# Cluster attention and two mixers on one core: grouping the v products, packing U's products, dividing the copies of turned exponentials two to one

## The chip, the cores and the metric

The kernel runs as one program on one core of a Trainium2 chip. The metric is the device time of one execution in microseconds; smaller is better. A time given below is a median over the runs shown, unless the text says that it is that of the profiled execution.

## What is computed

Inputs are q, k, v (2 batches, 8 heads, 768 positions, 64 channels), cluster centroids, and the weights of two mixer blocks. The first part is attention in which a query sees only the keys of its own cluster; its output, 2 x 768 x 512, goes through a low-rank token mixer and a wide channel mixer, and then through a second mixer pair.

```python
q_assign = argmax(q_n . c_n)                 # nearest centroid of each query, k_assign the same
mask   = q_assign[:, :, :, None] == k_assign[:, :, None, :]
scores = where(mask, q @ k.T / 8, -1e9)
x      = softmax(scores) @ v                 # 2 x 768 x 512
u      = x + U-V token mixer:  h = x.T @ U @ V,  u = x + h.T        (rank 32)
x2     = u + relu(u @ w_ch1) @ w_ch2         # hidden width 2048
...                                          # a second mixer: 256 over tokens, 1536 over channels
```

## The kernel before

The order of all work is written out by hand (a manual schedule): each engine runs its instructions in the order in which the program issues them, and a semaphore wait in front of one holds up everything behind it on that engine.

**Attention.** Heads are taken two at a time: G = 8 pairs (4 per batch). A pair has 12 score tiles of 128 queries by 768 keys (two halves of the queries, two heads, three tiles each), so there are 96 tiles, and `step(n)` issues tile n's share. For a tile, TensorE makes the scores (`s_mm`, four matmuls of 384 columns into two PSUM banks, issued two tiles ahead), VectorE finds the row maximum (`s_max`, L289), ScalarE exponentiates into the buffer `p32` (`s_exp`, L294), TensorE turns the six 128x128 blocks (`t_mm`, L311; "turned exponentials"), and every four turned blocks are one PSUM bank that VectorE or ScalarE copies to the buffer `pt` (`t_out`, L316 and L318). One and a half such groups come from a tile, so an even step begins a group (`i == 0`) and an odd step finishes one begun before it. Groups are numbered j; odd j went to VectorE and even j to ScalarE.

**The product with v.** Six tiles make a half k of a pair. While half k is made, the steps r = 0 to 5 of it issue `pv(k - 1, r)`: the product of key block r of the half before with v, for both heads, the two heads side by side in the array's columns (64 each) and accumulating in PSUM bank 7. After the sixth block ScalarE copies the bank to `osb` (`pv_out`, L326); two steps later TensorE turns it back (`merge`, L331) and VectorE divides by the row sums into `xn` (`merge_out`, L339).

**U's product.** When a pair is finished, `zmm(g)` computes U transposed times its part of x: six matmuls that fill 32 of the array's 128 columns. Two ScalarE casts and a VectorE subtraction (`zmm_out`, L354 to L356) store it as high part, high part, low part in `zst`. The last pair's runs after the attention loop in `rest_of_u`. `zadd` later adds V's product of it to x, six times per batch; for batch 0 in the loop, for batch 1 after it.

**What fixes the place of the rest.** The dictionaries `mid` and `late` hold work keyed by step: `mid` is TensorE work (merge, zmm, scores of clusters, zadd, turning of u), `late` what the other engines and the DMA queue do at the end of a step, among it the cluster assignment of the next pair, its loads, and from step 56 the conversion of the channel mixer's weights (`wide`, L96 to L109, L78, L85). PSUM banks 4 to 6 are handed out in turn by `ring()` to turned groups, merges, zmm and the like. The order inside a step was:

```python
if i == 0:   heads; run(mid); t_mm(0..4); pvs; maxima; t_mm(4..6); exps; t_out(j); pvo; run(late)
else:        t_mm(0..2); heads; maxima; t_mm(2..6); t_out(j); pvs; run(mid); exps; t_out(j+1); pvo; run(late)
```

Here `heads` is `s_mm(n+2)`, `maxima` is `s_max(n+2)`, `exps` is `s_exp(n+1)`.

**After the loop** come the last half's product with v (six blocks in a row), and the mixers as a stream of 512-column matmuls.

Of the kernel before, what the change touches and what calls it, by code (L numbers as in the profile page):

```python
# [9 lines left out]
F32 = mybir.dt.float32  # L10
# [8 lines left out]
P = 128  # L19
# [5 lines left out]
def tile_cluster_attention__then__two_mixers(  # L25
# [24 lines left out]
    pe, dve, act, pool, sp = nc.tensor, nc.vector, nc.scalar, nc.gpsimd, nc.sync  # L50
    NB, NPAIR, _, S = qT.shape
    HS = S // 2
    NS = S // P
    NT = HS // P
    D = 64
    CD = NPAIR * P
    NC = CD // P
    NFA, NFB = wa.shape[0], wb.shape[0]
    R = U.shape[1]
    DT = wt1.shape[1]  # L60
    NDT = DT // P
    G = NB * NPAIR
    NTT = 4 * NT
# [4 lines left out]
    const = ctx.enter_context(tc.tile_pool(name="const", bufs=1))  # L68
    psp = ctx.enter_context(tc.tile_pool(name="psp", bufs=1, space=bass.MemoryType.PSUM))
    ps = psp.tile([P, 8, 512], F32, name="ps")  # L70

    def mm(o, l, r, start, stop, **kw):
        pe.matmul(o, lhsT=l, rhs=r, start=start, stop=stop, **kw)  # L73

    def rnd(eng, o, i, scale=1.0):

        if eng is act:
            act.activation(o, i, AF.Copy, scale=scale)  # L78
        elif eng is dve and scale == 1.0:
            dve.tensor_copy(o, i)  # L80
        else:
            eng.tensor_scalar(out=o, in0=i, scalar1=scale, scalar2=1.0, op0=ALU.mult, op1=ALU.mult)

    def sub(eng, o, a, b):
        eng.tensor_tensor(out=o, in0=a, in1=b, op=ALU.subtract)  # L85

    f32 = lambda ap: ap.bitcast(F32)
# [35 lines left out]
    xn = fp.tile([P, NB, NPAIR, NS, P], F32, name="xn")  # L123
# [46 lines left out]
    u_sb = const.tile([P, NS, R], F32, name="u_sb")  # L170
    vst = const.tile([96, S], F32R, name="vst")
    zst = const.tile([96, NB * CD], F32R, name="zst")
    wcl = const.tile([P, 16], BF16, name="wcl")
    msk = const.tile([P, 2], F32, name="msk")

    def load_pair(g, eng=sp):
        b, p = divmod(g, NPAIR)
        eng.dma_start(Rq, qT[b, p])
        eng.dma_start(Rk, kT[b, p])
# [5 lines left out]
    held = {}  # L185

    def scores(g):
        p = g % NPAIR
        held["sc"] = bk = ring()
        for qd in range(4):  # L190
            src = (Rq, Rk)[qd // 2]
            mm(ps[32 * qd : 32 * qd + 32, bk, 0:HS], zc[:, ts(p, 32)], src[:, ts(qd % 2, HS)], True, True)
# [47 lines left out]
    def k_lo(eng, o):  # L240
        sub(eng, o.bitcast(F32R), Rk, Hk)
# [59 lines left out]
    def ring():  # L301

        banks.append(banks.pop(0))
        return banks[-1]

    def t_mm(n, c0, c1):
        for c in range(c0, c1):
            j, i = divmod(NS * n + c, 4)
            if i == 0:
                tb[j] = ring()  # L310
            pe.transpose(ps[:, tb[j], ts(i, P)], p32[n % NP32][:, ts(c, P)], ident)  # L311

    def t_out(j):
        o = pt[:, ts(j % NBL, 4 * P)]
        if j % 2:
            dve.tensor_copy(o, ps[:, tb[j], :])  # L316
        else:
            act.copy(o, ps[:, tb[j], :])  # L318

    def pv(q, c):  # L320
        for a in range(2):
            r = pt[:, ts((2 * q + a) % 4, NBL * P)].rearrange("p (t c k) -> p t c k", t=NT, c=NS)[:, :, c, :]
            mm(ps[D * a : D * a + D, OB, 0:HS], vr[q // 2 % 2][:, c, ts(a, D)], r, c == 0, c == NS - 1)
# [4 lines left out]
    def merge(q, bk=None):  # L328
        held["mg"] = bk = bk or ring()
        for t in range(NT):  # L330
            pe.transpose(ps[:, bk, ts(t, P)], osb[q % 2][:, ts(t, P)], ident)  # L331

    def merge_out(q):
        g, h = divmod(q, 2)
        b, p = divmod(g, NPAIR)
        r = rr[h]
        dve.tensor_scalar(out=r, in0=rs[q % 4], scalar1=EPS, scalar2=None, op0=ALU.add)
        dve.reciprocal(r, r)
        dve.tensor_tensor(  # L339
            out=xn[:, b, p, ts(h, NT), :].rearrange("p t (a d) -> p (t a) d", a=2),  # L340
            in0=ps[:, held["mg"], 0:HS].rearrange("p (x d) -> p x d", d=D),
            in1=r.unsqueeze(2).to_broadcast([P, 2 * NT, D]), op=ALU.mult)

    def zmm(g, bk):
        b, p = divmod(g, NPAIR)
        held["z"] = bk
        z = ps[0:R, bk, 0:P]
        for c in range(NS):
            mm(z, u_sb[:, c, :], xn[:, b, p, c, :], c == 0, c == NS - 1)

    def zmm_out(g):
        z = ps[0:R, held["z"], 0:P]
        o = zst[:, ts(g, P)]
        act.copy(o[0:32], z)  # L354
        act.copy(o[32:64], z)
        sub(dve, o[64:96], z, f32(o[0:32]))  # L356


    def zadd(b, t, bk):
        mm(ps[:, bk, :], vst[:, ts(t, P)], zst[:, ts(b, CD)], True, True)  # L360
# [211 lines left out]


    NTILE = G * NTT
    mid, late = {}, {}

    def at(d, s, f):
        d.setdefault(max(s, 0), []).append(f)

    for g in range(G):  # L580
        s0 = NTT * g
        for h in range(2):
            s = s0 + 2 * NT * h + 4 * NT + 1
            at(mid, s, lambda q=2 * g + h: merge(q))
            at(late, s, lambda q=2 * g + h: merge_out(q))
        if g + 1 < G:
            at(mid, s0 + NTT + 8, lambda g=g: zmm(g, ring()))
            at(late, s0 + NTT + 8, lambda g=g: zmm_out(g))
        n, s1 = g + 1, s0
        if 2 <= n < G:  # L590
            at(late, s1 - 8, lambda g=n: load_pair(g))
            at(mid, s1 - 5, lambda g=n: scores(g))
            at(late, s1 - 5, scores_out)
            at(late, s1 - 4, q_hi)
            at(late, s1 - 4, arg0)
            at(late, s1 - 3, lambda: arg1(pool))
            at(late, s1 - 2, k_hi)
            at(late, s1 - 2, arg2)
            at(late, s1 - 1, lambda: arg3(pool))
            at(late, s1 - 1, lambda: k_lo(pool, Rk))  # L600
            at(late, s1, arg4)
            at(late, s1, lambda: q_lo(dve, Rq))
            at(late, s1 + 1, lambda: mask_rows(pool))
            for what, s in (("hi", -2), ("lo", 1), ("mask", 2)):
                for a in range(2):
                    at(late, s1 + s, lambda g=n, a=a, w=what: stack(g, a, w, sp))
        if n < G:
            at(late, s1 + 6 if n > 1 else 1, lambda g=n: load_v(g))

    for t in range(NS):  # L610
        s = (59, 63, 69, 75, 81, 87)[t]

        def za(t=t):
            held["za"] = ring()
            zadd(0, t, held["za"])

        at(mid, s, za)
        at(late, s, lambda t=t: zadd_out(0, t, held["za"]))
# [24 lines left out]
    def step(n):  # L643
        k, r = divmod(n, 2 * NT)
        j, i = divmod(NS * n, 4)

        def run(d):
            for f in d.get(n, ()):
                f()

        def heads():
            if n + 2 < NTILE:
                s_mm(n + 2)

        def maxima():
            if n + 2 < NTILE:
                s_max(n + 2)

        def exps():
            if n + 1 < NTILE:  # L660
                s_exp(n + 1)

        def pvs():
            if k:
                pv(k - 1, r)

        def pvo():
            if k and r == 2 * NT - 1:
                pv_out(k - 1)

        if i == 0:
            heads()
            run(mid)
            t_mm(n, 0, 4)
            pvs()
            maxima()
            t_mm(n, 4, NS)
            exps()
            t_out(j)
            pvo()  # L680
            run(late)
        else:
            t_mm(n, 0, 2)
            heads()
            maxima()
            t_mm(n, 2, NS)
            t_out(j)
            pvs()
            run(mid)
            exps()  # L690
            t_out(j + 1)
            pvo()
            run(late)
# [178 lines left out]
    def rest_of_u():  # L872


        ops = [(lambda bk: zmm(G - 1, bk), lambda bk: zmm_out(G - 1))]
        u_, z_ = ([(f, o, b, t) for b in range(NB) for t in range(NS)] for f, o in ((umm, umm_out), (zadd, zadd_out)))
        order = u_[4:6] + z_[6:8] + u_[6:8]
        for i in range(8, 12):
            order += z_[i : i + 1] + u_[i - 1 : i] * (i > 8)
        order.append(u_[11])  # L880
        for f, o, b, t in order:
            ops.append((lambda bk, f=f, b=b, t=t: f(b, t, bk), lambda bk, o=o, b=b, t=t: o(b, t, bk)))
        for i in range(len(ops) + 1):
            if i:
                ops[i - 1][1](6 + (i - 1) % 2)
            if i < len(ops):
                ops[i][0](6 + i % 2)
            for _ in range((2, 1, 1, 2, 1, 1, 1)[i] if i < 7 else 4 if i > 7 else 12):
                yield
# [61 lines left out]
```

## Time and profile before

| | |
|---|---|
| median of 3 runs | 796.47 us (795.81 to 799.31) |
| the profiled execution | 796.2 us |
| its span in the profile | 794.1 us |
| busy, TensorE / VectorE / ScalarE / GpSimd | 760.7 / 488.4 / 305.6 / 156.5 us |
| attention loop, from the first product with v to the last merge | about 36 to 274 us of the span |

The profile is a page of one execution and a trace that can be asked for stretches, lines and waits. "PE" is TensorE's matmuls, "PEld" its weight loads, DVE VectorE, ACT ScalarE. fp32 matmuls appear as two records each, so a block of the product with v (two heads) is four records. The granted clock is TensorE's clock as a share of full speed. A row of a timeline that ends with a bracket tells how long the engine was idle before it and which instruction ended that.

### The profile page before, as it was taken

To read this page: it belongs to the slowest core of one execution; us is meant where nothing else is said; L and a number is where in the kernel's file an instruction comes from. 1 tells how busy PE (TensorE), PEld (TensorE's weight loads), DVE (VectorE), ACT (ScalarE), POOL (GpSimd) and SP (SyncE) were. 2 spreads that over 40 slices of the span, in tenths; PEclk is the share of its full clock that TensorE was granted. 3 is DMA by queue.
4 is the path that set the end of the run, shared out by engine and by line. 5 is a ranking of instruction groups with operands and counts; after the bars stand their busy time and mean duration, and the time that the engine had idled before them with its cause. 6 is when DMAs were issued, how large, how long until landed. Compare 5 with 4: busy or idle time off the path is not lost.

```text
span 794.1 us, 10612 instructions
## 1 busy us (share of the span) xinstructions
PE 760.7 (96%) x3845; PEld 584.4 (74%) x3845; DVE 488.4 (62%) x719; ACT 305.6 (38%) x563; POOL 156.5 (20%) x135
## 2 busy tenths in 40 slices
PE   1989999999999999899999999999999999999998
PEld 0655666666666677677788888888888888888886
DVE  5877767768877589695757887856682232114113
ACT  3566665666666444232323333323241210110110
POOL 3340430421400001141322222214411220000000
PEclk9999999999999999999999999999999999999999
DMA  5962644566621158999999899978775437555752
GB/s 148 214 128 81 139 113 129 126 207 152 165 92 54 54 212 292 392 368 353 391 386 326 302 392 375 377 282 277 267 282 206 134 133 246 203 187 169 273 193 80
DMA packets 59204, 176.66 MB, mean 222 GB/s; under 512 B 8625, under 2 KB 16817, under 8 KB 57105
## 3 DMA queue, kind: packets, MB, share of 16 engines
q1 hardware_dynamic: 58640, 175.27, 66.0%
q10 hardware_dynamic: 512, 0.72, 0.3%
q8 instruction: 30, 0.49, 0.2%
q14 instruction: 22, 0.17, 0.1%
HBM read 124.58 MB, written 32.51 MB: 198 GB/s over the span
## 4 chain that ended last, share of the span: by engine, by line
PE 86%; DMA 6%; DVE 3%; ACT 2%; issue 1%; ACTq 0%; SPq 0%; DVEq 0%
PE ps L73 76%; PE ps L311 8%; DMA qk<-scr_a 4%; PE ps L331 1%; DMA sk__80<-in_kT_dram 1%; DVE c__75 L106 1%; PE ps L823 1%; DVE c__75 L109 1%; DMA sq__79<-in_qT_dram 1%; ACT qk L78 1%; DMA qk<-sq__79 0%; PE ps L368 0%; ACT p L294 0%; DMA qk<-om 0%; DVE gl L729 0%
## 5 line engine op out<-in xcount | busy, mean ns | idle before, releaser
L73 PE MATMUL ps<-gh,qk 128*128 128x512 f32 x672 | 221.8, 391 | 3.3 <-DMA qk<-scr_a 3.2
L729 DVE SCALAR_TENSOR_TENSOR gl<-ps,gh 128x512 fp32r<-128x512 f32 x84 | 58.0, 690 | 190.7 <-ACT gh L728 190.7
L728 ACT ACTIVATE gh<-ps 128x512 fp32r<-128x512 f32 x84 | 50.2, 598 | 274.6 <-PE ps L73 274.1
L73 PEld LDWEIGHTS ps<-gh,qk 128*128 128x128 f32 x672 | 126.2, 188 | 30.6 <-ACT c__75 L96 2.7
L73 PE MATMUL ps<-qk 112*128 112x384 f32 (+2 forms) x492 | 119.6, 371 | 12.1 <-DMA qk<-om 9.7
L73 PE MATMUL ps<-gl,qk 128*128 128x512 f32 x336 | 130.9, 390 | 0.0
L289 DVE TENSOR_REDUCE nm<-ps 128x1 f32<-128x768 f32 x96 | 91.7, 955 | 41.0 <-PE ps L73 39.5
L73 PEld LDWEIGHTS ps<-qk 112*128 112x128 f32 (+1 forms) x492 | 84.6, 192 | 37.3 <-ACT p L294 14.3
L311 PEld LDWEIGHTS ps<-ident,p 128*128 128x128 f32 x576 | 67.0, 141 | 35.4 <-issue 19.3
L85 POOL TENSOR_TENSOR qk<-c__75,qk 128x512 fp32r<-128x512 f32 x34 | 49.1, 1449 | 222.9 <-ACT qk L78 220.3
L311 PE MATMUL ps<-ident,p 128*128 128x128 f32 x576 | 89.5, 278 | 2.4 <-ACT p L294 1.5
L294 ACT ACTIVATE p<-ps,nm 128x768 f32<-128x768 f32 x96 | 86.6, 902 | 11.2 <-DVE nm L289 10.6
L73 PE MATMUL ps<-pt,vr 128*64 128x384 f32 x384 | 82.1, 510 | 0.0
L73 PE MATMUL ps<-u1h,qk 128*128 128x512 f32 x224 | 73.9, 391 | 0.1
L73 PE MATMUL ps<-u2h,qk 128*128 128x512 f32 x224 | 73.9, 391 | 0.0
L73 PEld LDWEIGHTS ps<-gl,qk 128*128 128x128 f32 x336 | 63.1, 188 | 12.5
L318 ACT COPY pt<-ps 128x512 f32<-128x512 f32 x72 | 42.1, 585 | 70.7 <-PE ps L311 69.3
L73 PE MATMUL ps<-qk,qk 128*128 128x512 f32 x228 | 55.9, 394 | 1.0 <-DMA qk<-scr_a 1.0
L73 PEld LDWEIGHTS ps<-qk,qk 128*128 128x128 f32 x228 | 42.2, 188 | 10.0 <-DMA qk<-scr_a 1.4
L316 DVE COPY pt<-ps 128x512 f32<-128x512 f32 x72 | 49.0, 681 | 0.4 <-PE ps L311 0.4
L73 PEld LDWEIGHTS ps<-u1h,qk 128*128 128x128 f32 x224 | 42.0, 188 | 9.1 <-DMA qk<-scr_a 0.5
L73 PEld LDWEIGHTS ps<-u2h,qk 128*128 128x128 f32 x224 | 42.0, 188 | 8.6
(138 smaller groups left out, 906.9 us busy)
## 6 DMA issues: line engine op xcount, KB each, us to landing
qk<-scr_a SPq DMA_DIRECT2D x84, 512.0 KB, 7.9
qk<-scr_b SPq DMA_DIRECT2D x72, 512.0 KB, 4.2
c__74<-in_wa_dram SPq DMA_DIRECT2D x16, 1024.0 KB, 6.2
c__74<-in_wb_dram SPq DMA_DIRECT2D x24, 512.0 KB, 6.7
scr_b<-qk SPq DMA_DIRECT2D x24, 512.0 KB, 6.5
scr_a<-qk SPq DMA_DIRECT2D x22, 512.0 KB, 4.9
qk<-sq__79 SPq DMA_DIRECT2D x14, 384.0 KB, 4.0
qk<-sk__80 SPq DMA_DIRECT2D x28, 192.0 KB, 2.8
```

The source lines that it names most:

```text
L73: pe.matmul(o, lhsT=l, rhs=r, start=start, stop=stop, **kw)
L78: act.activation(o, i, AF.Copy, scale=scale)
L85: eng.tensor_tensor(out=o, in0=a, in1=b, op=ALU.subtract)
L106: dve.scalar_tensor_tensor(out=d, in0=lo, scalar=29, in1=d, op0=ALU.logical_shift_right, op1=ALU.bitwise_or)
L109: dve.scalar_tensor_tensor(out=d, in0=hi, scalar=-0x40000000, in1=d, op0=ALU.bitwise_and, op1=ALU.bitwise_or)
L289: dve.tensor_reduce(out=nm[:, n % 4 : n % 4 + 1], in_=ps[:, b0 : b0 + 2, 0:HS], axis=AX.XY, op=ALU.max, negate=True)
L294: act.activation(p32[n % NP32].rearrange("p (j k) -> p j k", j=2), ps[:, b0 : b0 + 2, 0:HS], AF.Exp, bias=nm[:, n % 4 : n % 4 + 1], accum_ ...
L311: pe.transpose(ps[:, tb[j], ts(i, P)], p32[n % NP32][:, ts(c, P)], ident)
L316: dve.tensor_copy(o, ps[:, tb[j], :])
L318: act.copy(o, ps[:, tb[j], :])
L728: act.activation(gh, o, AF.Relu)
L729: dve.scalar_tensor_tensor(out=gl, in0=o, scalar=0.0, in1=f32(gh), op0=ALU.max, op1=ALU.subtract)
```

## The change

Three edits, and a move that goes with the first. (1) `pv` is issued in odd steps alone, for two key blocks, r - 1 and r; in odd steps `mid` moves ahead of it, next to the transposes, and a new dictionary `low` (the cluster scores and `zmm`) runs right behind it. (2) `zmm` takes several pairs, each in its own 32 columns, at step 57 (pairs 0 to 3), step 93 (pairs 4 to 6) and after the loop (pair 7). Its results are first copied to `z32` (VectorE and ScalarE in turn) and then split for all pairs at once by `z_split` (two ScalarE roundings and one subtraction, in the two steps behind). The steps of `zadd` for batch 0 move from 59, 63, 69, 75, 81, 87 to 63, 65, 69, 71, 75, 77. (3) `t_out` gives every third group (j % 3 == 1) to VectorE and the others to ScalarE: 48 and 96 groups in all, where both had 72.

```diff
+    z32 = const.tile([32, CD], F32, name="z32")
...
     def t_out(j):
-        if j % 2:
+        if j % 3 == 1:
             dve.tensor_copy(o, ps[:, tb[j], :])
         else:
             act.copy(o, ps[:, tb[j], :])
...
-    def zmm(g, bk):
+    def zmm(gs, bk):
         held["z"] = bk
         for c in range(NS):
-            mm(z, u_sb[:, c, :], xn[:, b, p, c, :], c == 0, c == NS - 1)
+            for i, g in enumerate(gs):
+                b, p = divmod(g, NPAIR)
+                mm(ps[R * i : R * i + R, bk, 0:P], u_sb[:, c, :], xn[:, b, p, c, :], c == 0, c == NS - 1)
...
+    def zmm_out(gs):
+        for i, g in enumerate(gs):
+            z, o = ps[R * i : R * i + R, held["z"], 0:P], z32[:, ts(g % NPAIR, P)]
+            if i % 2:
+                act.copy(o, z)
+            else:
+                dve.tensor_copy(o, z)
+
+    def z_split(gs):
+        n, g = len(gs), gs[0]
+        z, o = z32[:, g % NPAIR * P : (g % NPAIR + n) * P], zst[:, g * P : (g + n) * P]
+        return [lambda: rnd(act, o[0:32], z), lambda: rnd(act, o[32:64], z), lambda: sub(dve, o[64:96], z, f32(o[0:32]))]
...
-            at(mid, s1 - 5, lambda g=n: scores(g))
+            at(low, s1 - 5, lambda g=n: scores(g))
...
+    for s, gs in ((57, range(NPAIR)), (93, range(NPAIR, G - 1))):
+        at(low, s, lambda gs=gs: zmm(gs, ring()))
+        at(late, s, lambda gs=gs: zmm_out(gs))
+        for i, f in enumerate(z_split(gs)):
+            at(late, s + (i + 3) // 2, f)
...
-        s = (59, 63, 69, 75, 81, 87)[t]
+        s = (63, 65, 69, 71, 75, 77)[t]
...
         def pvs():
             if k:
+                pv(k - 1, r - 1)
                 pv(k - 1, r)
...
             t_mm(n, 0, 4)
-            pvs()
             maxima()
...
             t_mm(n, 2, NS)
+            run(mid)
             t_out(j)
             pvs()
-            run(mid)
+            run(low)
             exps()
```

**Where the instructions stand.** First TensorE in the two steps of tiles 22 and 23 (qk are score matmuls, ident,p the turnings, pt,vr the product with v; here a matmul of either kind is one row entry). Before:

```order
L73 MATMUL ps<-qk_72 128x384 x4
L311 MATMUL ps<-ident,p_2_91 128x128 x4
L73 MATMUL ps<-pt,vr_88 64x384 x2
L311 MATMUL ps<-ident,p_2_91 128x128 x2
L311 MATMUL ps<-ident,p_3_92 128x128 x2
L73 MATMUL ps<-qk_72 128x384 x4
L311 MATMUL ps<-ident,p_3_92 128x128 x4
L73 MATMUL ps<-pt,vr_88 64x384 x2
```

The same two steps in the change:

```order
L73 MATMUL ps<-qk_72 128x384 x4
L312 MATMUL ps<-ident,p_2_91 128x128 x6
L312 MATMUL ps<-ident,p_3_92 128x128 x2
L73 MATMUL ps<-qk_72 128x384 x4
L312 MATMUL ps<-ident,p_3_92 128x128 x4
L73 MATMUL ps<-pt,vr_88 64x384 x4
```

The two groups of the product with v have become one, and tile 23's first two turnings follow those of tile 22 with nothing between.

Then ScalarE over three tiles (p buffers 0 to 2; L294 or L295 is the exponential, L318 or L319 the copy of a turned group). Before:

```order
L294 ACTIVATE p_0_89,rs_97<-ps,nm 128x768
L294 ACTIVATE p_1_90,rs_97<-ps,nm 128x768
L318 COPY pt<-ps 128x512
L294 ACTIVATE p_2_91,rs_98<-ps,nm 128x768
L318 COPY pt<-ps 128x512
```

In the change:

```order
L295 ACTIVATE p_0_89,rs_98<-ps,nm 128x768
L319 COPY pt<-ps 128x512
L295 ACTIVATE p_1_90,rs_98<-ps,nm 128x768
L319 COPY pt<-ps 128x512
L295 ACTIVATE p_2_91,rs_98<-ps,nm 128x768
L319 COPY pt<-ps 128x512
```

A copy now stands between any two exponentials.

Last, TensorE around U's product. Before, for one pair, in step 56:

```order
L73 MATMUL ps<-qk_72 128x384 x4
L73 MATMUL ps<-xn,u_sb 32x128 x6
L311 MATMUL ps<-ident,p_0_89 128x128 x4
L73 MATMUL ps<-pt,vr_87 64x384 x2
```

In the change, for four pairs, in step 57:

```order
L312 MATMUL ps<-ident,p_1_90 128x128 x4
L73 MATMUL ps<-pt,vr_87 64x384 x4
L73 MATMUL ps<-xn,u_sb 32x128 x24
L73 MATMUL ps<-qk_73 128x384 x4
```

It has moved from between scores and turnings to right behind the product with v.

## Rows read from the trace of the kernel before

**Rows 1.** The page, busy time of each engine.
```profile
PE 760.7 (96%) x3845; PEld 584.4 (74%) x3845; DVE 488.4 (62%) x719; ACT 305.6 (38%) x563; POOL 156.5 (20%) x135
```

**Rows 2.** Busy time by stretch: stretch, length, PE, PEld, DVE, ACT, POOL, clock, DMA.
```profile
48.00:284.00 236.00, 232.40 (x1442) 151.81 (x1441) 173.24 (x264) 147.12 (x290) 47.31 (x41) 1.00 0.46 119
```

**Rows 3.** Waits of TensorE, 20 to 284 us: total, times, longest.
```profile
PE ps L73 <- DMA sk__80<-in_kT_dram: 0.6, 1, 0.6
```

**Rows 4.** Timeline of PE, steps 16 and 17: start, length, engine, line, records.
```profile
62.24 0.98 PE L73 MATMUL ps<-qk 112*128 112x384 f32 x4
63.06 0.60 PE L311 MATMUL ps<-ident,p 128*128 128x128 f32 x4
63.59 0.87 PE L73 MATMUL ps<-pt,vr 128*64 128x384 f32 x4
64.38 0.66 PE L311 MATMUL ps<-ident,p 128*128 128x128 f32 x4
64.80 0.95 PE L73 MATMUL ps<-qk 112*128 112x384 f32 x4
...
66.12 0.87 PE L73 MATMUL ps<-pt,vr 128*64 128x384 f32 x4
66.91 0.97 PE L73 MATMUL ps<-qk 112*128 112x384 f32 x4
```

**Rows 5.** Timeline of PE behind the loop: the last half's six blocks.
```profile
276.12 4.09 PE L73 MATMUL ps<-pt,vr 128*64 128x384 f32 x24
280.14 0.98 PE L73 MATMUL ps<-qk 128*128 128x512 f32 x3
```

**Rows 6.** Timeline of PE at steps 2 and 3: eight turnings in a row.
```profile
29.09 1.03 PE L311 MATMUL ps<-ident,p 128*128 128x128 f32 x8
29.88 0.95 PE L73 MATMUL ps<-qk 128*128 128x384 f32 x4
```

**Rows 7.** Timeline of PE in a pair of steps with U's product.
```profile
74.59 0.96 PE L73 MATMUL ps<-qk 128*128 128x384 f32 x4
75.48 1.50 PE L73 MATMUL ps<-xn,u_sb 128*32 128x128 f32 x12
76.90 0.66 PE L311 MATMUL ps<-ident,p 128*128 128x128 f32 x4
...
80.81 0.98 PE L73 MATMUL ps<-qk 112*128 112x384 f32 x4
```

**Rows 8.** Timeline of PE: start of the cluster scores ahead of the row at 74.59.
```profile
73.80 0.52 PE L73 MATMUL ps<-sq__79,zc 128*32 128x384 f32 x2
```

**Rows 9.** Groups by shape, 20 to 420 us: count, busy, mean ns, idle before.
```profile
L289 DVE TENSOR_REDUCE nm<-ps 128x1 f32<-128x768 f32 x96 | 91.7, 955 | 41.0 <-PE ps L73 39.5 <-PE ps L311 0.9
L294 ACT ACTIVATE p<-ps,nm 128x768 f32<-128x768 f32 x96 | 86.6, 902 | 11.2 <-DVE nm L289 10.6
L316 DVE COPY pt<-ps 128x512 f32<-128x512 f32 x72 | 49.0, 681 | 0.4 <-PE ps L311 0.4
L318 ACT COPY pt<-ps 128x512 f32<-128x512 f32 x72 | 42.1, 585 | 70.7 <-PE ps L311 69.3 <-DVE qk L85 1.2
L78 ACT ACTIVATE qk<-c__75 128x1024 fp32r<-128x1024 f32 x6 | 6.3, 1057 | 2.6 <-DVE c__75 L109 2.6
```

**Rows 10.** Timeline of all engines at step 11: ScalarE's conversion of V's weights.
```profile
53.16 0.92 ACT L96 ACTIVATE xn<-xn 96x768 f32<-96x768 f32 x1
```

**Rows 11.** Timeline of all engines, steps 17 and 18: copy to osb, V's split, exponential, turning.
```profile
67.03 0.48 ACT L326 COPY osb<-ps 128x384 f32<-128x384 f32 x1 [0.22 <-PE ps L73]
67.41 2.54 ACT L78 ACTIVATE vst<-xn 32x768 fp32r<-32x768 f32 x3
...
69.97 0.90 ACT L294 ACTIVATE p<-ps,nm 128x768 f32<-128x768 f32 x1
...
71.02 0.44 PE L311 MATMUL ps<-ident,p 128*128 128x128 f32 x2 [1.53 <-ACT p L294]
```

**Rows 12.** Waits of TensorE, 284 to 794 us.
```profile
PE ps L73 <- DMA qk<-scr_a: 4.7, 4, 2.3
```

More of the change, by code (lines that the diff above doesn't have):

```diff
@@ L342, in merge_out @@
             in1=r.unsqueeze(2).to_broadcast([P, 2 * NT, D]), op=ALU.mult)
-    def zmm(g, bk):
-        b, p = divmod(g, NPAIR)
+    def zmm(gs, bk):
         held["z"] = bk
-        z = ps[0:R, bk, 0:P]
         for c in range(NS):
-            mm(z, u_sb[:, c, :], xn[:, b, p, c, :], c == 0, c == NS - 1)
[L351 to L356, printed above, removed]
+            for i, g in enumerate(gs):
[12 more added lines that the diff above has]
+        return [lambda: rnd(act, o[0:32], z), lambda: rnd(act, o[32:64], z), lambda: sub(dve, o[64:96], z, f32(o[0:32]))]
     def zadd(b, t, bk):
@@ L574, in tile_cluster_attention__then__two_mixers @@
     NTILE = G * NTT
-    mid, late = {}, {}
+    mid, low, late = {}, {}, {}
     def at(d, s, f):
@@ L585, in tile_cluster_attention__then__two_mixers @@
             at(late, s, lambda q=2 * g + h: merge_out(q))
-        if g + 1 < G:
-            at(mid, s0 + NTT + 8, lambda g=g: zmm(g, ring()))
-            at(late, s0 + NTT + 8, lambda g=g: zmm_out(g))
         n, s1 = g + 1, s0
@@ L872, in rest_of_u, with z_last @@
     def rest_of_u():
-        ops = [(lambda bk: zmm(G - 1, bk), lambda bk: zmm_out(G - 1))]
+        def z_last(bk):
+            zmm_out([G - 1])
+            for f in z_split([G - 1]):
+                f()
+        ops = [(lambda bk: zmm([G - 1], bk), z_last)]
         u_, z_ = ([(f, o, b, t) for b in range(NB) for t in range(NS)] for f, o in ((umm, umm_out), (zadd, zadd_out)))
```

## The prediction

> **What bounds the kernel now.** The page comes first: TensorE is busy 96% of the span [rows 1]. That number alone proves little, so the next view is the attention stretch, 48 to 284 us, where all three edits lie: TensorE 232.4 of 236 us, VectorE 173.2, ScalarE 147.1, at a granted clock of 1.00 throughout, the upper of its two levels (2.4 GHz) [rows 2]. The reader is to see two engines with room and one without. The view of waits agrees: from step 8 on TensorE's one long wait inside the loop is 1.53 us at step 18, where an exponential stands behind the split of V [rows 11]; the waits ahead of it belong to the start, where step 7 stands until a load of the next pair's keys has landed [rows 3]. So in the loop time is what TensorE's own sequence takes, and the timeline of two steps tells how it is made up.
>
> Two ordinary steps run from 62.24 to 66.91, 4.67 us [rows 4]. Scores to turnings take 0.82, four turnings to the product with v 0.53, that product 0.79, four turnings to the next scores 0.42 (they start at once, being behind an idle moment), then 1.32 over scores and turnings to the second product, and 0.79 for it. What the product costs by itself is told by the six blocks behind the loop: 276.12 to 280.14 is 4.02 us for six [rows 5], so with 0.79 for one alone a further block costs (4.02 - 0.79) / 5 = 0.645, and 0.15 of each lone block is the price of changing how the array is divided.
>
> **Edit 1, the product with v in every second step.** The new sequence is put together from the same rows: scores to turnings 0.82 [rows 4], eight turnings in a row 29.09 to 29.88, 0.79 [rows 6], scores and four turnings up to the product 1.32, two blocks 0.79 + 0.645 = 1.44 [rows 4, 5]. Sum 4.37, against 4.67: 0.30 less for two steps. Half is the second change of division, the other half that turnings behind a lone block are no longer restarted. This counts for steps 8 to 95, 44 pairs of steps: 44 x 0.30 = **13.2 us**. Steps 6 and 7 gain nothing, since step 7 ends with that load whenever TensorE arrives [rows 3]. Merges and zadd only swap one side of the product for the other, and the cluster scores lose a change of division (they take 0.79 to the scores behind, 73.80 to 74.59 [rows 7, 8]); I take zero for these.
>
> **Edit 2, U's product.** The two steps with it last 74.59 to 80.81, 6.22 us [rows 7], that is 1.55 more than 4.67. Seven such in the loop cost 10.9 us. In the change it runs twice, four and three pairs side by side. No row shows this shape side by side. The lower bound is that a group costs what a single one does, 75.48 to 76.90, 1.42 us [rows 7], with no further change of division since it stands behind the product with v; the upper bound is that the 48 and 36 records run one after another at 1.42 / 12 = 0.118, together 9.9 us. The nearest row speaks for the lower: the cluster scores put four 32-column products into the array, eight records of 384 fp32 columns, and are through in 0.79 us [rows 8], about one block of the product with v. So 2 x 1.42 = 2.8, and the gain is 10.9 - 2.8 = **8.1 us**; at the upper bound 1.0. The Trainium skill (TensorE: Matmul & The Clock Gate, Part 3, "Measured speedup vs the span model") is less kind: it gives three column tiles side by side 2.38 times the speed, not three. By that a group would cost about 3 / 2.38 = 1.26 of a single one, and the sum would be worse by 2 x 0.37 = 0.7 us, an estimate from that page; no run here shows it.
>
> The seven sets of small casts and subtractions become seven copies and two wide splits, on engines that are idle a quarter of the stretch or more [rows 2]. If that cover is gone they show as waits, counted next.
>
> **Edit 3 and the waits that the shorter sequence uncovers.** VectorE loses 24 copies of 0.681 and ScalarE gains 24 of 0.585, 16.3 and 14.0 us [rows 9]. ScalarE's load becomes 147 + 14 = 161 of some 215 us: no bound by sum. But its order is strict, and the exponential of an odd tile is now wanted sooner, since its turnings follow those of the tile before directly. Count from the start of the scores behind the product: they are wanted at 0.82 + 6/8 x 0.79 = 1.41. In an ordinary pair the maximum of that tile ends some 3.5 us after the earlier scores began (1.61 for scores and eight turnings, 0.95 for the next scores, 0.955 for the maximum [rows 4, 6, 9]), and with 1.05 from an exponential's start to the turning (69.97 to 71.02 [rows 11]) it is there at 4.6, where 4.37 + 1.41 = 5.8 is soon enough: 1.2 us ahead of need. The added copy stands in that gap or in the one before. So ordinary pairs cost nothing; the exceptions do:
> - Every sixth step, at the end of a half, the copy to osb stands ahead of it: it starts 0.12 behind the scores (67.03 against 66.91), holds ScalarE 0.38 (to 67.41), then 1.05: 1.55 against 1.41, a wait of 0.14, 14 times: 2.0 [rows 4, 11].
> - Step 11 has the 0.92 us conversion behind that copy: +0.8 [rows 10].
> - Step 17 has V's split there, 67.41 to 69.97: the wait is 1.55 + 2.56 - 1.41 = 2.7, of which 1.5 is there before: +1.1 [rows 11].
> - Steps 57, 59 and 93: copies that wait for U's product, a wide split, and at 93 a rounding of 1.06 [rows 9] behind both, ahead of the last exponential, with no scores left to cover it: 0.4, 0.6 and 1.6.
> - About 1.1 for steps in which VectorE's queued conversions delay a maximum (72, 84).
>
> Sum 7.6 us. Its bounds are 0 (slack suffices) and twice that.
>
> **Sum.** 796.2 - 13.2 - 8.1 + 7.6 = **782.5 us**, against the profiled execution, which lies 0.3 below the median shown. Behind the loop nothing is changed but one added copy before the last pair's split; the mixers' stream waits only 4.7 us for reloaded weights [rows 12], and those reloads are issued by the same steps, so it shifts as a whole; I take no gain or loss there.
>
> **The rivals.**
> *Slack suffices* (chance 0.18). The waits above are bounded by single rows, and the maxima may come earlier. Then 796.2 - 21.3 = 774.9. For it: TensorE hides nearly every conversion now [rows 2]. Against it: step 18 shows that a queue on ScalarE does reach TensorE [rows 11].
> *Copies bind* (0.10). ScalarE has two copies and two exponentials per pair of steps, each copy waiting for turnings and holding the next exponential. If that costs 0.2 us more in each of 44 pairs, 9 us are given back: 791. For it: ScalarE's copies already waited for TensorE before 70.7 us in all [rows 9], and such waits now hold an exponential each time. Against: the 1.2 us of slack. The Trainium skill (TensorEngine Tiling (Array Packing), "PSUM Bottleneck") warns of this: tiling speeds TensorE but not the evacuation of PSUM, which may become the limit. By that rule edits 1 and 2 would give back part of what they gain; the trace of before does not bear it out, since there the copies wait for TensorE (the same 70.7 us) and hardly ever the reverse.
> *Side by side is one after another* (0.06). U's product at its upper bound gains 1.0: 796.2 - 13.2 - 1.0 + 7.6 = 789.6. Against it: the cluster scores [rows 8].
> *Slower* (0.06). The loop that ties tile to tile becomes the bound: exponential to turning 1.05, two turnings to the next scores 0.21 (half of 0.42), the scores 0.95, the maximum 0.96: 3.2 us per pair of steps [rows 4, 9, 11]. A VectorE copy of 0.68 and a ScalarE copy of 0.59 in series make it 4.4. It decides from 4.37 + 21.3 / 44 = 4.85 on; with half of a 1.06 us row of other queued work in series too it is 4.97, which costs 44 x 0.60 = 26 us: 796.2 - 21.3 + 26 = 801. Against it: the added copies stand beside the maximum, not ahead of it, in the order shown.
>
> **How the numbers follow.** My forecast has 0.60, spread over 777 to 788. A measurement of this kernel tells about 0.5%, 4 us, from no change. Faster by more takes the forecast, the first and third rival and most of the second: 0.89; the rest of the second and a little of the fourth is the same, 0.06; slower 0.05. The range is 774 to 790.5: it holds the forecast, the first rival and the third, and leaves out the fourth and half of the second.
>
> **What would show it.** In the new profile the product with v should come in groups of eight records, 1.44 us to the next scores, an ordinary pair of steps should take 4.37, and U's product should appear in two groups of 48 and 36 records that last about 1.4 us each. TensorE's waits for the exponential should stand at every sixth step with 0.1 to 0.3 us, and at steps 18 and 94 with 2.7 and about 1.8. A pair of steps at 4.6 or more with waits for the exponential in each would make edit 1 wrong; a group of U's product at 4 us or more would make edit 2 wrong; a longer stretch behind the loop would make the rigid shift wrong.

## The result, and the profile after

| | before | after |
|---|---|---|
| median | 797.28 us (11 runs) | 789.88 us (788.53 to 793.91, 11 runs) |
| ratio, 95% interval | | 0.9912 (0.9894 to 0.993) |
| profiled execution / span | 796.2 / 794.1 us | 790.41 / 788.6 us |

The change is faster by 0.9%, about 7 us. The forecast was 13.7. Direction and range held; half of the expected gain is missing.

After's page gives TensorE 746.6 us of work (95% of the span), against 760.7 in [rows 1]. The attention stretch of after, beside [rows 2], shows that TensorE has less to do and is busy for a smaller part of it:

```profile
48.00:284.00 236.00, 224.11 (x1477) 157.61 (x1474) 166.48 (x250) 161.63 (x313) 48.46 (x42) 0.99 0.48 127
```

Before, TensorE stood idle for 3.6 of these 236 us; now 11.9. The waits of TensorE from 42 to 275 us (total, times, longest) say for what, first in before, then in after:

```profile
PE ps L311 <- ACT p L294: 1.5, 1, 1.5
PE ps L311 <- DVE qk L85: 0.8, 1, 0.8
```

```profile
PE ps L312 <- ACT p L295: 6.6, 5, 2.5
PE ps L312 <- DVE qk L85: 4.1, 4, 1.8
```

The sequence that the prediction put together is there nevertheless. Timeline of PE in after, steps 14 to 18, to be read against [rows 4]:

```profile
58.84 0.98 PE L73 MATMUL ps<-qk 128*128 128x384 f32 x4
59.65 1.04 PE L312 MATMUL ps<-ident,p 128*128 128x128 f32 x8
60.45 0.94 PE L73 MATMUL ps<-qk 128*128 128x384 f32 x4
61.23 0.60 PE L312 MATMUL ps<-ident,p 128*128 128x128 f32 x4
61.75 1.51 PE L73 MATMUL ps<-pt,vr 128*64 128x384 f32 x8
63.19 0.99 PE L73 MATMUL ps<-qk 112*128 112x384 f32 x4
...
67.58 0.98 PE L73 MATMUL ps<-qk 112*128 112x384 f32 x4
68.39 0.82 PE L312 MATMUL ps<-ident,p 128*128 128x128 f32 x6
71.68 0.44 PE L312 MATMUL ps<-ident,p 128*128 128x128 f32 x2 [2.47 <-ACT p L295]
71.87 1.22 PE L73 MATMUL ps<-qk 128*128 128x384 f32 x4
72.89 1.05 PE L312 MATMUL ps<-ident,p 128*128 128x128 f32 x4
...
74.52 2.11 PE L73 MATMUL ps<-pt,vr 128*64 128x384 f32 x8
76.56 0.52 PE L73 MATMUL ps<-sq__79,zc 128*32 128x384 f32 x2
```

A pair of steps takes 4.35 to 4.39 us (58.84 to 63.19, 63.19 to 67.58), eight records of the product with v 1.44: as forecast. Then comes step 18: a wait of 2.47, and behind it everything is slow. The scores to the next turnings take 1.02 instead of 0.78 to 0.80, the product with v 2.04 instead of 1.44. Busy time by stretch (columns as in [rows 2]; the clock is the third number from the right) gives the reason:

```profile
66.00:71.00 5.00, 3.21 (x20) 1.85 (x18) 1.78 (x3) 4.09 (x8) 0.00 (x0) 1.00 0.51 168
71.00:77.00 6.00, 5.32 (x29) 3.25 (x29) 4.02 (x7) 3.57 (x8) 0.00 (x0) 0.72 0.24 73
77.00:83.00 6.00, 6.00 (x45) 4.43 (x38) 3.78 (x6) 3.58 (x7) 2.92 (x3) 1.00 0.26 51
...
263.00:267.50 4.50, 3.92 (x15) 1.54 (x16) 1.78 (x5) 1.99 (x5) 0.00 (x0) 0.62 0.59 233
```

Behind the wait the granted clock is 0.72, so that for part of the stretch TensorE ran at the lower of its two levels, 1.2 GHz; from 77 us on it is 1.00 again. The last line is the stretch behind step 94, where the same happens. Timeline of PE there, and ahead of it the first group of U's product:

```profile
165.43 1.52 PE L73 MATMUL ps<-xn,u_sb 128*32 128x128 f32 x48
166.88 0.98 PE L73 MATMUL ps<-qk 112*128 112x384 f32 x4
167.69 0.82 PE L312 MATMUL ps<-ident,p 128*128 128x128 f32 x6
169.33 0.44 PE L312 MATMUL ps<-ident,p 128*128 128x128 f32 x2 [0.82 <-ACT p L295]
...
174.59 0.44 PE L312 MATMUL ps<-ident,p 128*128 128x128 f32 x2 [0.67 <-ACT p L295]
...
258.75 1.51 PE L73 MATMUL ps<-xn,u_sb 128*32 128x128 f32 x36
260.19 0.88 PE L312 MATMUL ps<-ident,p 128*128 128x128 f32 x6
262.99 1.09 PE L312 MATMUL ps<-ident,p 128*128 128x128 f32 x6 [1.92 <-ACT p L295]
264.01 2.83 PE L73 MATMUL ps<-pt,vr 128*64 128x384 f32 x8
```

Both groups of U's product last 1.44 to 1.45 to the next row, whether 48 records or 36; one pair alone took 1.42 [rows 7]. The second kind of wait, for `DVE qk L85`, stands where none was forecast: behind the turnings of u. The timeline of all engines at step 85 shows it best, first in after, then (TensorE alone) in before:

```profile
230.44 0.60 PE L375 MATMUL ps<-ident,xn 128*128 128x128 f32 x4
...
231.67 0.95 PE L73 MATMUL ps<-qk 128*128 128x384 f32 x4
232.00 1.12 ACT L96 ACTIVATE c__75<-c__74 128x1024 f32<-128x1024 f32 x1
233.01 0.59 ACT L78 ACTIVATE qk<-ps 128x512 fp32r<-128x512 f32 x1
...
233.64 0.69 DVE L85 TENSOR_TENSOR qk<-ps,qk 128x512 fp32r<-128x512 f32 x1 [1.97 <-ACT qk L78]
234.38 0.66 PE L312 MATMUL ps<-ident,p 128*128 128x128 f32 x4 [1.77 <-DVE qk L85]
```

```profile
241.88 0.60 PE L368 MATMUL ps<-ident,xn 128*128 128x128 f32 x4
...
242.84 0.87 PE L73 MATMUL ps<-pt,vr 128*64 128x384 f32 x4
...
245.84 0.66 PE L311 MATMUL ps<-ident,p 128*128 128x128 f32 x4 [0.84 <-DVE qk L85]
```

The turning of u (L375, L368 in before) takes a bank of the same ring of three (`ring()`) as the groups of turned exponentials do. The next two groups take the other two banks, so the third, which is the last four turnings of step 85, needs u's bank. That comes free only when VectorE's subtraction (`umm_out`, L85) has read it, which waits for ScalarE's rounding (L78), which stands behind a weight conversion (L96). All this is the same in before, and there too the bank is free 3.96 us after the turning of u began (241.88 to 245.84; in after 3.94, 230.44 to 234.38). What has changed is how soon TensorE wants it. In before step 84's product with v (242.84) stands between, and the four turnings are next in line 2.97 us after the turning of u; without it they are next after 2.02. So 0.84 has become 1.77, and steps 87, 89 and 91, which had no wait, have 0.76 to 0.77.

**Where the time is, by stretch.** From the starts of the scores at steps 8, 20, 32, 44, 56, 68, 80 and the first scores-like row behind the last half's 24 records (280.14 in before [rows 5], 273.98 in after); the last column is experiment e10, described below, which has nearly none of these waits.

| steps | before | after | e10 |
|---|---|---|---|
| 8 to 19 | 31.26 | 32.87 | 28.22 |
| 20 to 31 | 31.08 | 27.91 | 27.62 |
| 32 to 43 | 31.09 | 27.91 | 27.85 |
| 44 to 55 | 31.11 | 27.91 | 27.63 |
| 56 to 67 | 31.51 | 31.61 | 29.33 |
| 68 to 79 | 30.59 | 28.20 | 27.98 |
| 80 to the end of the loop | 50.17 | 53.10 | 46.50 |
| sum | 236.81 | 229.51 | 215.13 |

In undisturbed stretches the change gains 3.2 us per twelve steps; in the first, the fifth and the last it gives 4.6 back (1.6, 0.1 and 2.9). The loop of e10 is 21.7 shorter than that of before and 14.4 shorter than that of after. Those 14.4 are waits and what follows them; two of the waits before has too, shorter (the 1.53 at step 18 and the 0.84 at step 85).

### The profile page after: what moved, and what is told of

Read it like the earlier page. It is cut to its first block, busy times and chain, and to the rows that moved or that the text cites. A ratio compares the mean times of both kernels' runs of the same rounds, so it can differ in the third digit from the quotient of the medians.

```text
span 788.6 us, 10585 instructions
## 1 busy us (share of the span) xinstructions
PE 746.6 (95%) x3845; PEld 585.9 (74%) x3845; DVE 474.7 (60%) x695; ACT 317.5 (40%) x580; POOL 155.9 (20%) x135
## 4 chain that ended last, share of the span: by engine, by line
PE 86%; DMA 6%; DVE 3%; ACT 3%; issue 1%; ACTq 0%; SPq 0%; DVEq 0%
PE ps L73 77%; PE ps L312 8%; DMA qk<-scr_a 4%; DMA sk__80<-in_kT_dram 1%; ACT p L295 1%; PE ps L332 1%; DMA sq__79<-in_qT_dram 1%; ACT qk L78 1%; PE ps L834 1%; DVE c__75 L106 1%; PE ps L375 1%; DVE c__75 L109 0%; DVE qk L85 0%; DVE nm L290 0%; ACT vst L78 0%
## 5 line engine op out<-in xcount | busy, mean ns | idle before, releaser
L73 PE MATMUL ps<-qk 112*128 112x384 f32 (+2 forms) x492 | 120.5, 373 | 12.6 <-DMA qk<-om 10.5
L85 POOL TENSOR_TENSOR qk<-c__75,qk 128x512 fp32r<-128x512 f32 x34 | 49.1, 1451 | 226.8 <-ACT qk L78 212.8
L312 PE MATMUL ps<-ident,p 128*128 128x128 f32 x576 | 82.6, 276 | 10.8 <-ACT p L295 6.6
L295 ACT ACTIVATE p<-ps,nm 128x768 f32<-128x768 f32 x96 | 86.7, 903 | 9.6 <-DVE nm L290 8.3
L319 ACT COPY pt<-ps 128x512 f32<-128x512 f32 x96 | 56.1, 584 | 44.7 <-PE ps L312 43.9
L73 PE MATMUL ps<-pt,vr 128*64 128x384 f32 x384 | 74.0, 509 | 0.0
L73 PEld LDWEIGHTS ps<-gl,qk 128*128 128x128 f32 x336 | 63.5, 189 | 12.7
L96 ACT ACTIVATE c__75<-c__74 128x512 f32<-128x512 f32 (+2 forms) x47 | 38.5, 819 | 18.6 <-DMA c__74<-in_wa_dram 12.8
```

The lines of the kernel that those rows point to most:

```text
L96: act.activation(dst, hi.bitcast(F32), AF.Abs)
L295: act.activation(p32[n % NP32].rearrange("p (j k) -> p j k", j=2), ps[:, b0 : b0 + 2, 0:HS], AF.Exp, bias=nm[:, n % 4 : n % 4 + 1], accum_ ...
```

## The experiments

All times are medians of 4 to 12 runs, with the ratio to before and its interval. The unit of comparison is after's 0.9912. The theory at the outset: the edits gain what was forecast, and single waits at known steps give half of it back. The rivals: the copies of turned exponentials bind, U's product side by side costs more than one, or the loss lies behind the loop.

**e4, the copies shared evenly again.** Edit 3 undone.

```diff
-        if j % 3 == 1:
+        if j % 2:
             dve.tensor_copy(o, ps[:, tb[j], :])
```

> The copies of turned groups are divided half and half again; all else is as in the change. Theory A: ordinary pairs of steps have 1 us of slack on both engines and stay at 4.37; only the places with queued work shift between the engines: 789 to 791. Theory B (copies bind): without 24 copies on ScalarE the ordinary pairs and the waits for exponentials shrink, 5 us or more less, under 785.

790.47 us, 0.991 (0.9893 to 0.9927): no difference from after that the intervals could tell. ScalarE has 24 copies less and VectorE 24 more, and TensorE's waits for the exponential are the same 6.6 us, five times. The division of the copies is neither cost nor gain, and "copies bind" falls. The Trainium skill (TensorEngine Tiling (Array Packing), "PSUM Bottleneck") warns that copying out of PSUM may become the limit when tiling speeds TensorE up. The trace of after does not bear it out here, since ScalarE's copies still wait 43.9 us in all for TensorE:

```profile
L319 ACT COPY pt<-ps 128x512 f32<-128x512 f32 x96 | 56.1, 584 | 44.7 <-PE ps L312 43.9
```

**e2, V's split and conversion moved to even steps.** There scores, four turnings, the product with v and scores again stand between the queued work and the use of the next exponential. `vst_split` becomes a list of its four operations, one to a step.

```diff
...
-    for i, s in ((0, 6), (1, 11)):
+    for i, s in ((0, 6), (1, 12)):
...
-    at(late, 17, vst_split)
+    for s, f in zip((18, 24, 26, 28), vst_split):
+        at(late, s, f)
```

> Theory A: V's conversion and split stand on ScalarE behind the copy to osb, ahead of an exponential that TensorE wants, at steps 11 and 17: 0.95 and 2.7 us of wait, and after the longer one the granted clock reads 0.72 from 71 to 77 us, where a sequence of 4.69 us at full clock takes 1.6 more. With the conversion one step later and the split's three roundings in steps 18, 24 and 26, all go but the 0.15 us of the copy itself: about 5.0 us less, 785. Rival: the clock falls for the density of the whole stretch, not for this wait: the low stretch stays or comes elsewhere, and the gain is 3.4 us, 786.5. Theory B: no more than 1 us.

785.74 us, 0.9847 (0.9828 to 0.9865), 5.2 less than after. The waits of steps 12 and 18 are gone, but for the 0.15 of the copy to osb, and so is the low clock, which e4 still has. Busy time from 70 to 76 us, first e2, then e4:

```profile
70.00:76.00 6.00, 6.00 (x40) 3.58 (x38) 4.38 (x9) 3.42 (x8) 1.26 (x2) 1.00 0.28 92
```

```profile
70.00:76.00 6.00, 4.90 (x25) 3.35 (x29) 4.97 (x8) 3.52 (x8) 0.00 (x0) 0.72 0.03 8
```

The two waits, 0.95 and 2.70 by the sequence, each with that 0.15 in it, do not make 5.2; the slow rows behind the second (71.87 to 76.56, 4.69, where the same rows take 3.1 at a clock of 1.00) supply 1.6.

**e1 and e5, the turnings of u at another place.** e1 has them in odd steps ahead of the product with v; e5 in odd steps behind it, so that 3.2 us pass from a turning of u to the next use of its bank (233.53 to 236.74 below) instead of 2.0.

```diff
-        at(mid, NTILE - 12 + 2 * t, um)
-        at(late, NTILE - 12 + 2 * t, lambda t=t: umm_out(0, t, held["um"]))
+        at(low, NTILE - 11 + 2 * t, um)
+        at(late, NTILE - 11 + 2 * t, lambda t=t: umm_out(0, t, held["um"]))
```

This is e5; e1 has `mid` in place of `low`.

> Theory A (single waits): most of what the prediction missed sits in a few places where TensorE waits. One is steps 85 to 91, where the turned tile's last group needs the PSUM bank that the turning of u took in the same pair of steps and waits for u's subtraction: 1.77 + 3 x 0.76 us of waits, 4.7 us by the sequence (once 1.92, three times 0.93). Moved to the odd steps, behind the tile's last group, these four waits go: about 785.2 us, and ordinary pairs of steps stay at 4.37. Theory B (copies bind): the two-to-one division of the copies costs in every pair, the waits named are only where it shows: no gain beyond 1 us, 789 to 790.

> As the first experiment, but the turning of u stands behind the product with v of the odd steps, where every bank it takes has been copied. Theory A: the four waits for u's subtraction are gone, 4.7 us less than the change: 785.2. Rival: the first experiment's gain came from its reading other data or banks too early, and in a sound order the bank is simply waited for elsewhere: 789 to 790.

e1: 785.28 us, 0.9847 (0.9827 to 0.9866). It computes something else: in two steps (85 and 91) the merge and the turning of u both take a bank there, and the second bank is one whose turned exponentials have not been copied yet. So its time is only a hint. e5 is free of that: 787.08 us, 0.9867 (0.985 to 0.9883), 3.6 less than after, against 4.7 expected. In both the waits for `DVE qk L85` have gone. In e5's trace steps 84 to 91 take 21.1 us, in after's 24.8, which is the same 3.7. Most of the missing 1 us is a new small wait in each of the four; timeline of PE in e5:

```profile
233.53 0.66 PE L375 MATMUL ps<-ident,xn 128*128 128x128 f32 x4
...
235.76 0.44 PE L312 MATMUL ps<-ident,p 128*128 128x128 f32 x2 [0.21 <-ACT p L295]
...
236.74 0.60 PE L312 MATMUL ps<-ident,p 128*128 128x128 f32 x4
```

Its waits for the exponential are 7.4 us in nine, where after has 6.6 in five.

**e6, the splits of U's product in even steps, its copies on VectorE alone.**

```diff
-            if i % 2:
-                act.copy(o, z)
-            else:
-                dve.tensor_copy(o, z)
+            dve.tensor_copy(o, z)
...
-            at(late, s + (i + 3) // 2, f)
+            at(late, s + ((1, 5, 5) if s < 90 else (1, 2, 2))[i], f)
...
-        s = (63, 65, 69, 71, 75, 77)[t]
+        s = (65, 69, 71, 75, 77, 81)[t]
```

> All copies of U's product go to VectorE, and the wide roundings of the first group to steps 58 and 62, so that ScalarE meets none of it between an odd tile's maximum and its exponential. Theory A: the waits at steps 58 and 60 (1.05 and 0.90 us) shrink to the 0.15 of the copy to osb, and the wait at step 94 (2.2 us) with the low clock behind it (1.6 us) goes, since the rounding of 1.06 us no longer stands behind a copy that waits: 5 us less, 785. Rival: the rounding alone is long enough, and step 94 keeps a wait of 1 us or more and sometimes the low clock: 787 to 788.

784.85 us, 0.9839 (0.9817 to 0.986), 5.8 less than after. The eight turnings behind the first group run through again (timeline of PE in e6; in after they were broken by 0.82), and TensorE's waits for the exponential are down to the 3.2 us of steps 12 and 18:

```profile
166.72 1.04 PE L312 MATMUL ps<-ident,p 128*128 128x128 f32 x8
167.51 0.96 PE L73 MATMUL ps<-qk 112*128 112x384 f32 x4
```

After's lost time at steps 58, 60 and 94 is 1.05, 0.90 (0.15 of it the copy to osb) and 2.2 by the sequence, and 1.5 more in the slow rows behind 262.99: 5.65.

**e3, no second group inside the loop.** Pairs 4 to 6 join pair 7 behind it.

```diff
-    for s, gs in ((57, range(NPAIR)), (93, range(NPAIR, G - 1))):
+    for s, gs in ((57, range(NPAIR)),):
...
-            zmm_out([G - 1])
-            for f in z_split([G - 1]):
+            zmm_out(range(NPAIR, G))
+            for f in z_split(range(NPAIR, G)):
...
-        ops = [(lambda bk: zmm([G - 1], bk), z_last)]
+        ops = [(lambda bk: zmm(range(NPAIR, G), bk), z_last)]
```

> U's product of pairs 4 to 6 is taken out of step 93 and made together with pair 7's behind the loop. Theory A: gone are the group itself (1.44 us), the wait for the last exponential behind its copies and the rounding (2.2 us) and the low clock that follows (0.62 from 263 to 267.5 us, about 1.6 us): 5 us less, 785. Rival: behind the loop the four copies and the wide splits are short of cover, V's product for batch 1 comes late and holds the first mixer matmuls: 2 us less or no gain.

787.57 us, 0.9871 (0.9853 to 0.9889), 3.3 less than after: between theory and rival. The first row behind the last half's product stands at 268.40 instead of 273.98, of which 1.0 is an earlier start of the loop; but the stretch from there to the span's end has grown from 514.6 to 517.7. The waits of TensorE there (268 to 790 us) include the two below; after has none of the second kind and 3.4 us of the first, of which before has 4.7 [rows 12]:

```profile
PE ps L73 <- DMA qk<-scr_a: 4.9, 3, 2.4
PE ps L73 <- DVE u1l L85: 0.9, 1, 0.9
```

So of the 4.6 us by which the loop of e3 is shorter than after's (224.9 against 229.5), 3.1 come back behind it: taking the product out of the loop moves most of the loss instead of curing it.

**e8, edit 2 alone, and e11, edit 1 alone**, both with the copies shared evenly. e8 is after with the product with v put back into every step and `mid` behind it in odd steps; the edit to `t_out` is that of e4.

```diff
...
-    mid, low, late = {}, {}, {}
+    mid, late = {}, {}
+    low = mid
...
-                pv(k - 1, r - 1)
                 pv(k - 1, r)
...
             t_mm(n, 0, 4)
+            pvs()
...
-            run(mid)
             t_out(j)
             pvs()
-            run(low)
+            run(mid)
```

e11 makes the opposite edit in before.

> U's product in groups alone, on the order of before: product with v in every step, copies half and half. Theory A: it brings its 8.1 us nearly whole, for in the old order the exponential of the odd tile had 0.8 us more room: 789 to 790, so that the change's other edits, net of their waits, brought about nothing. Rival: the groups' copies make their waits (4 us) in any order: 793.

> The product with v in every second step alone, on before: U's product pair by pair, copies half and half. Theory A: 13.2 us of TensorE time are saved and most of them are lost again in the single waits: 2.0 behind the copies to osb, 0.8 at step 12, 1.1 and the low clock's 1.6 at step 18, 4.7 at the turnings of u: 10.2, so about 3 us less than before, 794. Rival: these waits need the other two edits as well, and the edit alone brings 8 us or more: 789 or less.

e8: 791.87 us, 0.9932 (0.9916 to 0.9948), 5.4 less than before, between theory and rival. From step 20 to 55 its stretches of twelve steps take 29.48 to 29.49, 1.6 less than in before, which is one product of U, as forecast. Its trace has two waits for the exponential, 2.5 us in all, of which before has the 1.5 at step 18; the rest of the shortfall was not followed up. With the product with v in every step, its wait for `DVE qk L85` is one of 0.8, as in before. e11: 796.88 us, 0.9984 (0.9969 to 0.9998), 1.3 less than before where about 3 were expected: next to nothing of the 13.2 us by which the edit shortens the sequence. Its ordinary pairs do take 4.38. Waits of TensorE from 42 to 275 us:

```profile
PE ps L311 <- ACT p L294: 3.4, 3, 2.5
PE ps L311 <- DVE qk L85: 3.2, 4, 1.8
PE ps L311 <- DVE zst L85: 1.9, 7, 0.3
```

That is 8.5 us, against 2.3 in before for the first two; the third is the bank of U's product for a single pair, taken in the ring as the turnings of u take theirs, and the pairs of steps with it last 6.4 (steps 20, 32, 44, 56), where that of [rows 7] lasts 6.22. Add 0.15 in each of 14 halves and a low clock behind step 18 (0.74 from 70 to 76 us). The two edits' measured gains, 5.4 and 1.3, add up to about after's 7.

**e7, the three remedies together** (the edits of e2, e5 and e6), and **e9**, e7 with the copies shared evenly (the edit of e4).

> The second, the fifth and the sixth kernel's edits together. Theory A: the single waits add up, 4.7 + 5.0 + 5 us: 775, near the 774.9 that the prediction gave for the case in which slack suffices. Theory B (something common to all pairs of steps binds): the gains don't add, and it stays at 780 or above.

> The seventh kernel with the copies of turned groups half and half again. Theory A: with the single waits gone the division decides nothing in an ordinary pair (1 us of slack on either engine): 778, within 1.5 us. Theory B: the two-to-one division still costs, now that nothing hides it: 775 or less. The reason a designer could have had for it, that VectorE is the short engine: 781 or more.

e7: 778.08 us, 0.9753 (0.9736 to 0.977), 12.7 less than after, though 3 above the 775 expected; the single remedies sum to 14.6 (5.2 + 3.6 + 5.8), which three intervals of about 1.5 us each do not tell from 12.7. By the loops of the profiles the three are worth 4.6, 2.8 and 5.2, together 12.6, and e7 12.0. Waits of TensorE, 42 to 275 us: of the exponential's 6.6 ahead of turnings 0.8 are left, at the turnings of u.

```profile
PE ps L312 <- ACT p L295: 0.8, 4, 0.2
```

The clock from 70 to 76 us is 1.00. e9: 778.07 us, 0.9752 (0.9732 to 0.9773). Even with the waits gone, the division of the copies decides nothing.

**e10, also the copy to osb moved**, into the first step of the next half, behind that step's exponential, on top of e7.

```diff
-            if k and r == 2 * NT - 1:
-                pv_out(k - 1)
+            if k > 1 and r == 0:
+                pv_out(k - 2)
...
+    pv_out(last - 1)
     merge(last - 1, 4)
```

> The seventh kernel with the copy to osb moved from the end of a half to the next step, behind that step's exponential. Theory A: the last regular wait, 0.15 us behind that copy at every half, goes: 2 us less than 778, 776. Rival: the copy then holds the next group's exponential and nothing is gained: 778.

775.08 us (772.88 to 775.94), 0.9705 (0.9682 to 0.9728): 3.8 less than e7 and e9 by the ratios, 3.0 by the medians. The eight turnings behind the end of a half are through in 0.79 again (timeline of PE in e10); in after and e7 they take 0.94.

```profile
85.96 1.03 PE L312 MATMUL ps<-ident,p 128*128 128x128 f32 x8
86.75 0.94 PE L73 MATMUL ps<-qk 128*128 128x384 f32 x4
```

14 times 0.15 is 2.1; its loop is 2.4 shorter than e7's (215.1 against 217.5). This kernel beats both before, by 3.0%, and after.

## Why the prediction was right in direction and wrong in size

- **The bound** held: TensorE's own sequence. **Edit 1** and **edit 2** as sums held too. The pair takes 4.35 to 4.39 (4.37 forecast), U's product 1.45 and 1.44 per group (about 1.4). Three undisturbed stretches of twelve steps gain 3.2 each; the terms give 6 x 0.30 and 1.55 for one product of U, less 0.14 at the ends of two halves, 3.07. e10's loop is 21.7 shorter than before's, against 13.2 + 8.1 = 21.3. That this is so close is partly luck: before's own waits of 1.53 and 0.84 are gone in e10 too, and it has 0.8 of its own, so that the edits by themselves gave nearer to 20.
- **The Trainium skill's figure for column tiles** (TensorE: Matmul & The Clock Gate, Part 3, "Measured speedup vs the span model", 2.38 for three) did not show here: three pairs side by side take 1.44 and four 1.45, one alone 1.42, so the speed is 2.96 and 3.92 times. The page's row is for 512 columns, these products have 128. The measurement decides.
- **The step that failed is "Edit 3 and the waits that the shorter sequence uncovers", its sum of 7.6 us.** Its mechanism was right (single waits, no general one), its size half of what came: of the 21.3 us of the two edits 7.3 arrived in the loop (236.81 against 229.51), so 14.0 were lost there. By places, against what was forecast. As in the forecast, the 0.15 of the copy to osb is counted in the first row alone; and what before itself loses, read from the sequence in the same way (1.7 at step 18, 1.0 at step 85), is taken off:

| place | forecast | measured | shown by |
|---|---|---|---|
| copy to osb, 14 times | 2.0 | 2.1 | e10 |
| step 12, conversion | 0.8 | 0.8 | e2 |
| step 18, beyond before's wait | 1.1 | 0.8 | e2 |
| low clock behind step 18 | none | 1.6 | e2 |
| behind U's groups (steps 58, 60, 94) | 2.6 | 4.0 | e6 |
| low clock behind step 94 | none | 1.5 | e6 |
| maxima late behind VectorE's conversions (72, 84) | 1.1 | none seen | after |
| turnings of u (steps 85, 87, 89, 91) | none | 3.7 | e5, e8, e11 |

  The sum is 14.5, 0.5 above the 14.0. Most of the miss is two terms that the sum did not have. The first is u's bank. The prediction asked when an exponential is ready, but not when the bank is free that a turning writes to, and both are wanted sooner by the same edit: with no product with v between, the turnings come about 0.95 us earlier to a bank that comes free no earlier. Where the product stays in every step (before, e8) the waits of this kind are one of 0.8; where it is grouped (after, e11) there are four. The waits of before showed that one, and the prediction passed it over when it called the wait at step 18 the one long one. The second, the low clock, is a consequence of a wait that was itself forecast to 0.1 us.
- **The rows that "would show it"** came as said at steps 18 (2.70 by the sequence) and 94 (2.2, forecast about 1.8), with 0.15 at the ends of halves.
- **The rigid shift** held: 513.96 us from the end of the loop to the end of the span before, 514.62 after. The start of the loop is 1.1 later in after's profile (44.47 against 43.33), but in the profiles of the experiments it lies anywhere from 43.2 to 44.5, so this is not the change's.
- **The rivals.** "Slack suffices" (774.9) is what e7 and e10 make true by moving work, not what the change did. "Copies bind" fell with e4 and e9. "Side by side is one after another" fell with the rows at 165.43 and 258.75. The slower one did not come: ordinary pairs have no wait. (The 70.7 us for which ScalarE's copies are said to wait for TensorE are 69.3 in [rows 9], the rest being a wait for VectorE; nothing hangs on it.)

## What to carry to other kernels

When a hand-ordered sequence is tightened, cost the typical step and then list every step that has something extra, and for each both the work queued ahead on the producing engine and the moment at which the buffer is free that the next item takes out of a shared ring. A small wait that the kernel before already has is where to look first, since a tighter sequence makes it longer. A gain that is measured right in undisturbed stretches and is missing in the total sits in those few steps; moving their extra work to the step with more slack brought 16.5 us more here (e10), where the change itself had brought 7. What the same moves would do to the kernel before was not tried; its own two waits are 2.4 us. And a wait on TensorE may cost more than its length.

## What was not expected of the hardware

**A wait that slows what comes behind it.** In every profile with the 2.47 us wait at step 18 (after, e1, e3, e4, e5, e6, e11) the granted clock of the 6 us from 70 or 71 us on, around and behind its end, is 0.72 to 0.74, and from 77 us on it is 1.00 again; where the wait is 1.5 (before, e8) or absent (e2, e7, e10) it is 1.00. The price at step 18 is 1.6 us on top of 2.5. At step 94 the wait is 1.92 in after, e1, e2, e4 and e5, and the same eight records of the product with v behind it take 2.83, 2.83, 2.78, 1.51 and 2.57: in e4 the clock did not fall (1.00 from 263 to 267.5 us), though the rows ahead of the wait, from step 92 on, take the same times as in after. Each of these is a single execution. So the wait alone does not decide it; what else does stays open, as it was not tried.

**Copies out of one bank by two engines in turn.** `zmm_out`'s four copies of 0.26 to 0.28 us alternate between VectorE and ScalarE, yet each starts only when the one before has ended; timeline of all engines in after:

```profile
167.08 0.28 DVE L358 COPY z<-ps 32x128 f32<-32x128 f32 x1 [1.80 <-PE ps L73]
167.40 0.26 ACT L356 COPY z<-ps 32x128 f32<-32x128 f32 x1 [2.19 <-DVE z L358]
167.69 0.28 DVE L358 COPY z<-ps 32x128 f32<-32x128 f32 x1 [0.32 <-ACT z L356]
168.00 0.26 ACT L356 COPY z<-ps 32x128 f32<-32x128 f32 x1 [0.35 <-DVE z L358]
```

Each of the last three is released by the copy before it, so the program's own waits put them in a row. Copies of two turned groups out of two banks do run at the same time (164.60 on VectorE and 164.62 on ScalarE, both into `pt`), so the shared bank is the likely reason; that was not tried. Two engines gain nothing over one here: the four copies take 1.18 us, and 1.18 in e6, where VectorE makes all of them. And the exponential on ScalarE starts behind the last of them, at 168.29, although its maximum ended at 164.69; in e6 it starts at 164.11, and the turnings that need it no longer wait.
